# Attention on one Trainium2 core: GpSimd's two divisions of a pair of tiles as one two-array step

## The chip, the core and the metric

One core of one Trainium2 chip runs the whole program in one launch. The metric is the device time in microseconds, the median of three runs: 733.76 us before (733.6 to 734.52). An execution under the hardware profiler gives the rows that are quoted. Names in them: PE is TensorE (matmul), PEld its weight loads, DVE is VectorE, ACT is ScalarE, POOL is GpSimd, SP is SyncE; `L777` is line 777 of the kernel.

## The reference

Three blocks follow each other: windowed attention, a normalised feed-forward block with a residual, and a gated block with a short convolution. Only the first is touched by the change.

```
scores = scale * q @ k^T                     # 4 batches, 8 heads, 576 positions, 64 columns
scores = where(0 <= i - j < 128, scores - slope_h * |i - j|, -1e9)
attn   = exp(scores - max(scores))
attn   = attn / (sum(attn) + 1e-9)           # the division in question
x      = attn @ v                            # to (4, 576, 512)
x      = x + relu(layer_norm(x) * g @ w1) @ w2
h      = relu(x @ w_in);  out = (h * sigmoid(conv3(h))) @ w_out
```

## The kernel before

The 576 positions of two batches make nine tiles of 128 rows, the middle one half of each batch. With 2 pairs of batches, 4 pairs of heads and 9 tiles there are 72 tiles of two heads each; the kernel takes them in pairs (36), and two pairs, `a` and `b`, in each turn of its main loop (18 turns).

For a pair TensorE turns q and k (`turn_qk`, `L711`), and makes the scores of two tiles and two heads against 256 keys (`scores`, `L737`). Since the window is 128 wide, each row keeps just one of the two keys that lie 128 apart: VectorE joins the two halves with a mask (`join`, `L748`) and takes the minimum of the negated scores (`minima`, `L752`). ScalarE makes the exponentials, one step for each tile and head, and their sums (`exponentials`, `L762`). Then comes `shares`: VectorE adds 1e-9 (`L770`), takes the reciprocal (`L771`), and the four arrays of 128 columns are multiplied by their reciprocals, the two of the even head by VectorE (`L775`, one step of 256 columns), the two of the odd head by GpSimd (`L777`, two steps of 128 columns). The shares lie as `pp[row, tile, head, 128]`, so one head's two arrays are 256 columns apart, and its two reciprocals two columns apart.

After that TensorE turns the shares (`turn_p`, `L787`), ScalarE copies them from PSUM (`copy_p`, `L792`), GpSimd makes the two masked halves (`select_p`, two steps of 512 columns, `L799`), TensorE multiplies by v (`values`, `L815`), and ScalarE stores the result as x (`outputs`, `L828`).

Beside attention the same engines turn weights of the feed-forward block into the form that TensorE wants: GpSimd rescales (`L358`), VectorE shifts and merges bits (`L373`, `L378`, `L383`) and makes a low part (`L415`), ScalarE a high part (`L412`). Towards the end of attention the first layer norm is made too: GpSimd subtracts the mean (`L507`, 384 columns), VectorE makes low parts (`L449`).

Each engine takes its instructions in the order in which the program issues them, written out by hand in the main loop for this part of the kernel; between engines they wait on semaphores. `shares(b)` of one turn is issued in the middle of the next one, `shares(a)` at its own turn's end. A planner with costs and due times sets the order of the later blocks alone.

Of the kernel before, what the change touches and what calls it, by code (L numbers as in the profile page):

```python
# [14 lines left out]
ALU = mybir.AluOpType  # L15
PSUM = bass.MemoryType.PSUM

P = 128
# [192 lines left out]
def tile_kernel(  # L211
# [28 lines left out]
    V, S, G, T = nc.vector, nc.scalar, nc.gpsimd, nc.tensor  # L240
# [296 lines left out]
    with ExitStack() as actx:  # L537
# [110 lines left out]
        def blhs_f(kind: int, a: int = 0):  # L648
            return blhs[:, kind, a:].bitcast(F32)

        V.tensor_scalar(
            out=blhs[:, 0, :], in0=cf[:, P:W], scalar1=er[0], scalar2=er[1], op0=ALU.mult, op1=ALU.add
        )
        V.tensor_scalar(out=cb[:, 3:4], in0=er[0], scalar1=-1.0, scalar2=None, op0=ALU.mult)
        for i, r, base in ((1, 2, 3), (2, 3, 3), (0, 4, 1)):
            V.scalar_tensor_tensor(
                out=cb[:, i : i + 1], in0=er[r], scalar=BIG, in1=cb[:, base : base + 1],
                op0=ALU.mult, op1=ALU.add,
            )
        for i in range(4):  # L660
            cs = slice(i * D, (i + 1) * D)
            V.tensor_scalar(
                out=b0[:, cs], in0=cf[:, cs], scalar1=er[1], scalar2=cb[:, i : i + 1],
                op0=ALU.mult, op1=ALU.add,
            )
        for kind, r in ((1, 2), (3, 4)):
            V.tensor_scalar(
                out=blhs[:, kind, :], in0=blhs_f(0), scalar1=er[r], scalar2=None, op0=ALU.add
# [3 lines left out]
            out=blhs[:, 2, TAIL:], in0=blhs_f(0, TAIL), scalar1=er[2], scalar2=er[3],  # L672
            op0=ALU.add, op1=ALU.add,
        )
        for pr in range(NPAIR):
            V.tensor_scalar(
                out=brhs[:, pr, :], in0=b0, scalar1=sl[:, pr : pr + 1], scalar2=None, op0=ALU.mult
# [24 lines left out]
        live = {}  # L702
# [64 lines left out]
        def shares(n: int):  # L767

            sm = live["sm", n]
            V.tensor_scalar(out=sm[:, 1], in0=sm[:, 0], scalar1=1e-9, scalar2=None, op0=ALU.add)  # L770
            V.reciprocal(out=sm[:, 1], in_=sm[:, 1])  # L771
            pp = live["pp", n].rearrange("p u h j -> p (u h) j")
            even = live["pp", n][:, :, 0, :]
            r = sm[:, 1].rearrange("p (u h) -> p u h", h=2)[:, :, 0:1].broadcast_to([P, 2, P])
            V.tensor_tensor(out=even, in0=even, in1=r, op=ALU.mult)  # L775
            for i in (1, 3):
                G.tensor_scalar(  # L777
                    out=pp[:, i, :], in0=pp[:, i, :], scalar1=sm[:, 1, i : i + 1], scalar2=1.0,
                    op0=ALU.mult, op1=ALU.mult,
                )  # L780

        def turn_p(n: int, pool=ps_t, tag="pt"):
            pp = live.pop(("pp", n))
# [78 lines left out]
        for n in range(0, NS, 4):  # L862
# [21 lines left out]
            if n > 4:  # L884
                shares(b - 4)
# [4 lines left out]
            exponentials(a)  # L890
            exponentials(b, range(2 if 0 < n and not last else 4))
            shares(a)
            if not before:
                shares(b)
# [716 lines left out]
    for s in (1, 2):  # L1611
# [6 lines left out]
        for p in range(NF1 // 2):  # L1618
            extra = []
            if s == 1:  # L1620
                g, j = 4 + p // 4, p % 4
# [297 lines left out]
```

## Time and profile before

| | before |
|---|---|
| median of three runs | 733.76 us |
| the profiled execution | 733.1 us |
| its span | 731.4 us |
| TensorE busy | 711.1 us (97%) |
| VectorE busy | 518.9 us (71%) |
| ScalarE busy | 403.1 us (55%) |
| GpSimd busy | 242.7 us (33%) |
| granted TensorE clock, mean | 0.998 |

The span is what the profile covers; the time of the execution lies 1.7 us above it. Busy times are means over very different stretches: attention fills the first 147 us, and all of GpSimd's divisions and selects lie there. A busy TensorE is not one at its peak, and the duration of a GpSimd or VectorE step holds whatever the step waited for after it had started.

### The profile page before, as it was taken

How to read it: one execution, taken by the hardware profiler on the slowest of the kernel's cores; microseconds unless marked ns; L12 is line 12 of the kernel's file. 1: busy time of each engine (PE TensorE's matmuls, PEld its weight loads, DVE VectorE, ACT ScalarE, POOL GpSimd, SP SyncE). 2: the span in 40 equal slices, each digit the busy share in tenths (PEclk: the TensorE clock that was granted, in tenths of full speed). 3: DMA queues.
4: the chain of work that ended last, by engine and by line, in shares of the span. 5: the costliest groups of instructions: out<-in, count | busy, mean ns of one | idle time of the engine just before them, and what ended most of it. 6: DMA issues, size and time to landing. Idle time of an engine off the chain costs nothing.

```text
span 731.4 us, 13425 instructions
## 1 busy us (share of the span) xinstructions
PE 711.1 (97%) x4704; PEld 663.3 (91%) x4704; DVE 518.9 (71%) x1017; ACT 403.1 (55%) x1050; POOL 242.7 (33%) x408
## 2 busy tenths in 40 slices
PE   7999988899999999999999999999999999999998
PEld 6777866799999999999999999999999899998887
DVE  6799899577888636566778655468469998786731
ACT  4888877654534323344346334344477787776741
POOL 1788889868822102221310223343421000000000
PEclk9999999999999999999999999999999999999999
DMA  6777766258539827977860689997932000000011
GB/s 152 174 184 178 193 161 188 70 159 239 172 112 293 266 70 205 304 220 246 249 190 11 190 273 290 295 276 208 261 93 81 16 30 16 30 21 23 30 49 53
DMA packets 122303, 114.63 MB, mean 157 GB/s; under 512 B 63552, under 2 KB 87292, under 8 KB 122236
## 3 DMA queue, kind: packets, MB, share of 16 engines
q1 hardware_dynamic: 101020, 76.81, 35.1%
q0 software_dynamic: 20160, 36.71, 18.2%
q8 instruction: 37, 0.61, 0.3%
q10 hardware_dynamic: 1056, 0.26, 0.2%
q14 instruction: 30, 0.25, 0.1%
HBM read 80.70 MB, written 33.05 MB: 156 GB/s over the span
## 4 chain that ended last, share of the span: by engine, by line
PE 83%; POOL 6%; DVE 5%; ACT 3%; DMA 2%; issue 1%; POOLq 0%; ACTq 0%; DVEq 0%
PE bank L1038 73%; PE ps L737 3%; POOL pt L799 2%; DMA wind<-r 2%; PE po L815 2%; POOL pp L777 2%; PE ptp L787 2%; PE ptr L711 1%; DVE ps L748 1%; DVE mn L752 1%; PE bank L1094 1%; ACT fa L999 1%; POOL xm L507 1%; ACT pp L762 1%; PE busy L611 1%
## 5 line engine op out<-in xcount | busy, mean ns | idle before, releaser
L1038 PE MATMUL bank<-hhr,r 128*128 128x384 f32 x1152 | 213.8, 337 | 0.5 <-DVE fa L1006 0.5
L1038 PE MATMUL bank<-r,r 128*128 128x288 f32 (+1 forms) x1248 | 204.0, 314 | 1.2 <-ACT fa L999 1.2
L1038 PEld LDWEIGHTS bank<-hhr,r 128*128 128x128 f32 x1152 | 199.1, 188 | 2.6 <-DVE fa L1006 1.5
L1038 PEld LDWEIGHTS bank<-r,r 128*128 128x128 f32 x1248 | 193.9, 188 | 4.4 <-ACT fa L999 2.3
L1332 POOL DMA_DIRECT2D r<-w1d x96 | 51.8, 540 | 174.3 <-PE bank L1038 161.9
L999 ACT ACTIVATE fa<-bank 128x288 f32<-128x288 f32 (+1 forms) x112 | 49.8, 444 | 72.5 <-PE bank L1038 71.2
L1038 PE MATMUL bank<-r 128*128 128x512 f32 (+2 forms) x360 | 81.8, 372 | 0.2 <-ACT r L1782 0.2
L1038 PEld LDWEIGHTS bank<-r 128*128 128x128 f32 x360 | 63.6, 188 | 9.9 <-ACT r L1782 0.7
L999 ACT ACTIVATE r<-fa 128x256 fp32r<-128x256 f32 (+2 forms) x94 | 47.9, 521 | 39.0 <-DMA wind<-r 14.4
L1006 DVE TENSOR_TENSOR fa<-bank,fa 128x288 f32<-128x288 f32 (+1 forms) x88 | 43.5, 501 | 25.1 <-ACT fa L999 13.5
L999 ACT ACTIVATE hhr<-bank 128x384 fp32r<-128x384 f32 x46 | 22.5, 490 | 69.4 <-PE bank L1038 69.3
L777 POOL TENSOR_SCALAR pp<-pp,sm 128x128 f32<-128x128 f32 x72 | 48.7, 686 | 27.9 <-DVE sm L771 26.4
L762 ACT ACTIVATE pp<-ps,mn 128x128 f32<-128x128 f32 x144 | 51.4, 383 | 11.1 <-DVE mn L752 8.8
L1014 DVE SCALAR_TENSOR_TENSOR fa<-fa,cw 128x576 f32<-128x576 f32 x64 | 51.3, 814 | 1.5 <-ACT fa L999 0.7
L1006 DVE TENSOR_TENSOR r<-fa,r 128x256 fp32r<-128x256 f32 (+1 forms) x74 | 37.7, 521 | 20.1 <-ACT r L999 14.2
L1014 DVE SCALAR_TENSOR_TENSOR hhr<-bank,hhr 128x384 fp32r<-128x384 f32 x46 | 25.5, 554 | 33.9 <-ACT hhr L999 33.7
L737 PE MATMUL ps<-kt,qt 64*128 64x256 f32 x288 | 44.9, 406 | 2.6 <-ACT pp L762 1.7
L815 PE MATMUL po<-pt,rawv 128*64 128x128 f32 x544 | 38.2, 280 | 8.0 <-POOL pt L799 5.1
L1038 PE MATMUL bank<-r,hhr 128*128 128x512 f32 (+1 forms) x192 | 44.5, 381 | 0.0
L799 POOL TENSOR_SCALAR_AFFINE_SELECT pt<-pc 128x512 f32<-128x512 f32 x72 | 43.8, 639 | 1.5 <-ACT pc L792 1.0
L815 PEld LDWEIGHTS po<-pt,rawv 128*64 128x64 f32 x544 | 28.9, 136 | 17.0 <-POOL pt L799 14.3
L999 ACT ACTIVATE fa<-fa 128x576 f32<-128x576 f32 (+1 forms) x64 | 39.0, 620 | 2.5 <-DVE fa L1006 1.4
(146 smaller groups left out, 1129.7 us busy)
## 6 DMA issues: line engine op xcount, KB each, us to landing
r<-w1d POOLq DMA_DIRECT2D x96, 256.0 KB, 4.9
fa<-in_moe_w_ch SPq DMA_DIRECT2D x24, 512.0 KB, 5.3
w1d<-r SPq DMA_DIRECT2D x40, 256.0 KB, 3.7
wind<-r SPq DMA_DIRECT2D x28, 256.0 KB, 5.8
r<-wind POOLq DMA_DIRECT2D x28, 256.0 KB, 5.1
out<-h SPq DMA_DIRECT2D x17, 256.0 KB, 2.0
rawq<-in_q SPq DMA_DIRECT2D x32, 128.0 KB, 3.5
rawv<-in_v SPq DMA_DIRECT2D x32, 128.0 KB, 2.9
```

The costliest lines, as they stand in the source:

```text
L507: G.tensor_tensor(out=y, in0=xt(g * GT, (g + 1) * GT, j), in1=bcs[g, 0], op=ALU.subtract)
L737: T.matmul(ps[:, h, u, :].rearrange("p (o j) -> p o j", o=2), lhs, rhs, start=i == 0, stop=i == 1,)
L762: S.activation(pp[:, u, h, :], sc[:, h, u], AF.Exp, bias=mn[:, h, u : u + 1], scale=-1.0, accum_out=sm[:, 0, i : i + 1],)
L777: G.tensor_scalar(out=pp[:, i, :], in0=pp[:, i, :], scalar1=sm[:, 1, i : i + 1], scalar2=1.0, op0=ALU.mult, op1=ALU.mult,)
L787: T.transpose(ptp[:, 2 * u + h, :], pp[:, u, h, :], ident)
L799: G.affine_select(out=parts[:, i], in_=pc, compare_op=ALU.is_ge, fill=0.0, base=base, pattern=[[0, 4], [sign, P]], channel_multiplier=-sign,)
L815: T.matmul(po[h * D : (h + 1) * D, u, :], rvs[bl, pr][:, t - 1 + i, h, :], pt[:, i, 2 * u + h, :], start=i == i0, stop=i == 1,)
L999: lambda: S.activation(now(out), now(src), func, **kw),
L1006: "V", tt_ns(cols(out)), lambda: V.tensor_tensor(out=out, in0=a, in1=b, op=op),
L1014: lambda: V.scalar_tensor_tensor(out=now(out), in0=now(a), scalar=sc, in1=now(b), op0=op0, op1=op1),
L1038: T.matmul(out, lhs, now(rhs), start=start and n == 0, stop=stop and n == len(items) - 1, skip_group_check=True,)
L1332: plan.add("G", 560, lambda: nc.gpsimd.dma_start(dst, src), [src], [dst], nbytes=262144)
```

## The change

In `shares` GpSimd's two steps of 128 columns with a scalar for each row become one step of 256 columns with two arrays: the odd head's shares of both tiles, and their reciprocals, each repeated over 128 columns. It is the form that VectorE has for the even head already; a loop over the two engines now writes both. The arithmetic is the same.

```diff
-            pp = live["pp", n].rearrange("p u h j -> p (u h) j")
-            even = live["pp", n][:, :, 0, :]
-            r = sm[:, 1].rearrange("p (u h) -> p u h", h=2)[:, :, 0:1].broadcast_to([P, 2, P])
-            V.tensor_tensor(out=even, in0=even, in1=r, op=ALU.mult)
-            for i in (1, 3):
-                G.tensor_scalar(
-                    out=pp[:, i, :], in0=pp[:, i, :], scalar1=sm[:, 1, i : i + 1], scalar2=1.0,
-                    op0=ALU.mult, op1=ALU.mult,
-                )
+            for h, eng in enumerate((V, G)):
+                part = live["pp", n][:, :, h, :]
+                r = sm[:, 1].rearrange("p (u h) -> p u h", h=2)[:, :, h : h + 1].broadcast_to([P, 2, P])
+                eng.tensor_tensor(out=part, in0=part, in1=r, op=ALU.mult)
```

GpSimd's queue at the two turns that the prediction works through (from 102.4 us on), before; `pp` are the shares, `sm` the sums and reciprocals, `fa` a weight, `xm` the layer norm's differences, `pt` the masked halves, and the numbers are those of the buffers:

```order
L777 TENSOR_SCALAR pp_1618<-pp_1618,sm_1619 128x128 x2
L358 TENSOR_SCALAR fa<-fa 128x512
L777 TENSOR_SCALAR pp_1730<-pp_1730,sm_1731 128x128 x2
L799 AFFINE_SELECT pt_1752<-pc_1750 128x512 x2
L799 AFFINE_SELECT pt_1818<-pc_1816 128x512 x2
L777 TENSOR_SCALAR pp_1736<-pp_1736,sm_1737 128x128 x2
L358 TENSOR_SCALAR fa<-fa 128x512
L507 TENSOR_TENSOR xm_0_1837<-x,fa 128x384
L777 TENSOR_SCALAR pp_1856<-pp_1856,sm_1857 128x128 x2
```

The same place of GpSimd's queue in the changed kernel, whose lines behind the edit are numbered five lower:

```order
L775 TENSOR_TENSOR pp_1594<-pp_1594,sm_1595 128x2x128
L358 TENSOR_SCALAR fa<-fa 128x512
L775 TENSOR_TENSOR pp_1704<-pp_1704,sm_1705 128x2x128
L794 AFFINE_SELECT pt_1725<-pc_1723 128x512 x2
L794 AFFINE_SELECT pt_1791<-pc_1789 128x512 x2
L775 TENSOR_TENSOR pp_1710<-pp_1710,sm_1711 128x2x128
L358 TENSOR_SCALAR fa<-fa 128x512
L507 TENSOR_TENSOR xm_0_1809<-x,fa 128x384
L775 TENSOR_TENSOR pp_1828<-pp_1828,sm_1829 128x2x128
```

Each two steps became one in the same place, and nothing else of this queue moved; VectorE's, ScalarE's, TensorE's and SyncE's queues hold the same instructions in the same order as before. In the changed kernel `L775` is the line of VectorE's and of GpSimd's division alike.

## Rows read from the trace of the kernel before

**Rows 1.** The page: the span, and the chain that ended last by engine.

```profile
span 731.4 us, 13425 instructions
...
PE 83%; POOL 6%; DVE 5%; ACT 3%; DMA 2%; issue 1%; POOLq 0%; ACTq 0%; DVEq 0%
```

**Rows 2.** Busy us and instructions by engine in two stretches; clock, DMA, GB/s.

```profile
20.00:147.00 127.00, 117.06 (x1226) 94.11 (x1224) 107.74 (x226) 101.08 (x401) 108.25 (x165) 1.00 0.66 163
147.00:731.40 584.40, 579.05 (x3380) 556.63 (x3377) 399.41 (x754) 292.48 (x610) 129.75 (x218) 1.00 0.51 155
```

**Rows 3.** The chain of waits, 100 to 127 us: start, us, engine, line.

```profile
106.62 0.61 DVE ps L748
...
113.43 1.39 POOL pp L777 x2
```

**Rows 4.** The chain of waits over the whole span: by line, three pieces.

```profile
by line: PE bank L1038 73.2%; PE ps L737 2.8%; POOL pt L799 2.4%; DMA wind<-r 2.4%; PE po L815 2.0%; POOL pp L777 1.8%; PE ptp L787 1.6%; PE ptr L711 1.2%; DVE ps L748 1.1%; issue 1.0%; DVE mn L752 0.9%; PE bank L1094 0.9%; ACT fa L999 0.8%
...
41.54 0.71 DVE ps L748
...
46.66 1.72 POOL pp L777 x2
...
134.10 1.37 DVE xna L449 x2
```

**Rows 5.** GpSimd's division by source line: shortest/middle/longest in ns.

```profile
L777 POOL TENSOR_SCALAR pp<-pp,sm x72: 364/535/1387, 13.0 to 139.1; 128x128 f32<-128x128 f32 x72
```

**Rows 6.** GpSimd's two-array steps by source line, the same columns.

```profile
L507 POOL TENSOR_TENSOR xm<-x,fa x4: 1002/1223/1460, 112.0 to 124.2; 128x384 f32<-128x384 f32 x4
L1236 POOL TENSOR_TENSOR r<-fa,r x20: 1299/1316/1762, 151.0 to 205.0; 128x512 fp32r<-128x512 f32 x20
```

**Rows 7.** Timeline of GpSimd, 102.4 to 115.2 us: start, us, instruction.

```profile
102.70 1.47 POOL L777 TENSOR_SCALAR pp<-pp,sm 128x128 f32<-128x128 f32 x2 [1.53 <-DVE sm L771]
104.14 0.90 POOL L358 TENSOR_SCALAR fa<-fa 128x512 f32<-128x512 f32 x1
105.02 1.83 POOL L777 TENSOR_SCALAR pp<-pp,sm 128x128 f32<-128x128 f32 x2
...
111.97 1.46 POOL L507 TENSOR_TENSOR xm<-x,fa 128x384 f32<-128x384 f32 x1
113.41 1.41 POOL L777 TENSOR_SCALAR pp<-pp,sm 128x128 f32<-128x128 f32 x2
```

**Rows 8.** Timeline of GpSimd, 102.4 to 103.75 us: a pair's first step alone.

```profile
102.70 1.12 POOL L777 TENSOR_SCALAR pp<-pp,sm 128x128 f32<-128x128 f32 x1 [1.53 <-DVE sm L771]
```

**Rows 9.** Timeline of VectorE, 102.4 to 115.2 us.

```profile
102.98 0.68 DVE L378 SCALAR_TENSOR_TENSOR fa<-fa 128x512 int32<-128x512 int32 x1
103.58 0.27 DVE L770 TENSOR_SCALAR sm<-sm 128x4 f32<-128x4 f32 x1
...
104.09 0.43 DVE L775 TENSOR_TENSOR pp<-pp,sm 128x256 f32<-128x256 f32 x1
104.44 1.14 DVE L415 TENSOR_TENSOR r<-fa,r 128x512 fp32r<-128x512 f32 x1
105.50 0.68 DVE L383 SCALAR_TENSOR_TENSOR fa<-fa 128x512 int32<-128x512 int32 x1
...
111.39 1.17 DVE L415 TENSOR_TENSOR r<-fa,r 128x512 fp32r<-128x512 f32 x1
112.48 1.49 DVE L383 SCALAR_TENSOR_TENSOR fa<-fa 128x512 int32<-128x512 int32 x1
113.90 0.41 DVE L373 TENSOR_SCALAR fa<-fa 128x512 int32<-128x512 int32 x1
```

**Rows 10.** Timelines of GpSimd and VectorE around 80.9 us.

```profile
80.88 0.67 POOL L358 TENSOR_SCALAR fa<-fa 128x512 f32<-128x512 f32 x1 [0.47 <-DMA fa<-in_moe_w_ch]
80.96 0.86 DVE L775 TENSOR_TENSOR pp<-pp,sm 128x256 f32<-128x256 f32 x1
```

**Rows 11.** Timeline of VectorE, 97 to 99.5 us: a join behind TensorE.

```profile
99.18 0.70 DVE L748 COPY_PREDICATED ps<-own,ps 128x512 f32<-128x512 int32 x1 [0.60 <-PE ps L737]
```

## The prediction

> **What bounds the kernel now.** I read the page's head first: TensorE is on 83% of the chain that ended last, GpSimd on 6%, VectorE on 5%, of 731.4 us [rows 1]. The change touches only attention, so next come the stretches. From 147 us to the end TensorE is busy 579.05 of 584.40 us; nothing of the change lies there, and it only starts earlier or later. From 20 to 147 us VectorE is busy 107.74 of 127 us and GpSimd 108.25 [rows 2]: two engines at 85%, neither with much slack, beside a TensorE that waits now and then. Whatever moves the end of this stretch moves the end of the kernel one for one, because no gap behind it is large enough to swallow it.
>
> The chain inside the stretch changes hands about every 7 us, once for each step of four tiles. In some steps it runs through VectorE up to the join (`L748`), in some through GpSimd's divisions (`L777`) and selects, in some it waits for TensorE's scores [rows 3, 4, 11]. `L777` is 1.8% of the whole chain, 13.2 us [rows 4]: of 36 pairs of divisions some nine are on it. So two questions count: how long GpSimd needs for a pair, and how long it keeps VectorE waiting meanwhile.
>
> **What a division waits for now.** `L777` takes 364 ns at best, 535 in the middle, 1387 at worst [rows 5]. The spread is waiting for VectorE, and the two timelines show it as an exclusive turn. The first division of the pair at 102.70 lasts 1.12 us, to 103.82 [rows 8]. It starts while VectorE's own division runs, and VectorE's next step `L378` also goes ahead of it, to 102.98 + 0.68 = 103.66 [rows 9]; the GpSimd step ends 0.16 us later. The second then ends at 102.70 + 1.47 = 104.17 [rows 7], so after its turn comes, the pair needs 0.51 us. The block works the other way too: `L770`, which handles four columns, starts at 103.58 and ends at 103.85, 0.03 us after the first division lets go [rows 9].
>
> **The change, part by part.** 72 one-array steps of 128 columns go; 36 two-array steps of 256 columns come, at the same places in GpSimd's queue. No DMA, queue, buffer or other engine's instruction moves.
>
> 1. The new step alone. The trace has GpSimd multiplying or subtracting two arrays at 384 and 512 columns: at best 1.002 and 1.299 us [rows 6]. That is (1.299 - 1.002) / 128 = 2.3 ns a column, so 256 columns take 1.002 - 128 x 0.0023 = 0.71 us. Two old steps at their best take 2 x 0.364 = 0.73 us [rows 5]. Alone, nothing is gained; the saved start is paid back by the second array.
>
> 2. The new step after a wait. The subtraction `L507` at 111.97 (384 columns) ends at 113.43, and VectorE's `L415` ahead of it ended at 111.39 + 1.17 = 112.56 [rows 7, 9]: 0.87 us of holding. For 256 columns I scale to 0.87 x 256 / 384 = 0.58 us. The bounds: if the repeated divisor costs nothing and the step goes at the rate of a one-array step, `L358` gives 0.52 us for 512 columns (it ends at 104.14 + 0.90 = 105.04, and VectorE's division ahead of it at 104.09 + 0.43 = 104.52) [rows 7, 9], so 0.26 us; if the repeated operand is dear, the 0.87 us of the 384 columns. No row shows a repeated operand on GpSimd. I take 0.58, the nearest two-array row. Against 0.51 for the old pair that is +0.07 us for GpSimd; in pairs whose second division had to wait as well (at 105.02, 1.83 us [rows 7]) it is a gain.
>
> [...]
>
> 3. What VectorE loses. Before, it was let in between the two divisions after 0.16 us; now it waits 0.58. `L770` ends 0.42 us later, and with it the next reciprocal and VectorE's next division.
>
> Worked through the step from 102.4 us. GpSimd's new step ends at 103.66 + 0.58 = 104.24 (before 104.17). VectorE's second division starts at 104.51 instead of 104.09, and now `L358`, started at about 104.21, is in front of it; alone `L358` takes 0.67, so until 104.88, and the division ends 0.27 us after it (as at 80.96 + 0.86 = 81.82 behind 80.88 + 0.67 = 81.55 [rows 10]), at 105.15 instead of 104.52. `L415` goes next, 0.60 us (as `L383` took: 105.50 + 0.68 = 106.18 behind 104.44 + 1.14 = 105.58 [rows 9]), to 105.75. Then GpSimd's second new step, to 106.33: before it was 105.02 + 1.83 = 106.85, so GpSimd is 0.52 us ahead. `L383` waits for that and ends 0.54 later (as behind `L507`: 112.48 + 1.49 = 113.97 against 113.43), at 106.87 instead of 106.18, and `L373` ends at 107.21 instead of 106.62: +0.59 us. The chain runs through VectorE here, straight into the join [rows 3]. So the step loses 0.59 us although GpSimd wins.
>
> The next step is GpSimd's: the first new step ends 0.07 late, `L358` wins back 0.24 because VectorE is now behind it, but `L507` lets VectorE's `L415` pass and ends 0.15 late, and the second new step, after `L373` as today (113.90 + 0.41 [rows 9]), ends at 0.15 + 0.07 = 0.22 us after 113.41 + 1.41 = 114.82 [rows 7].
>
> 4. The sum over the stretch, by who holds the chain. VectorE straight into the join, like 41.54 and 106.62 [rows 3, 4]: four steps, counting two where TensorE's scores come at about the same moment, so 0.5 each: +2.0. GpSimd with a weight step or `L507` between the pairs: three steps at 0.22: +0.66. GpSimd with a second division that waited, at 46.66: its two new steps come out about 0.25 ahead: -0.25. The step after 134.10, where VectorE's `L449` leads into the divisions and would be blocked [rows 4]: +0.4. TensorE's steps, where VectorE has been idle for it before the join, 0.60 us at 99.18 [rows 11]: VectorE has the room, 0. Together +2.8 us.
>
> The profiled execution took 733.1 us around its span of 731.4; the sum makes it 735.9. The median of the three runs is 733.76, so I predict 736.6.
>
> **Rivals.**
> - Faster: the new step runs near 0.26 us, since its divisor is two values repeated. For it: nothing in the trace has such an operand. Against: both two-array rows agree on 2.3 ns a column. Each of the nine pairs on the chain then gains 0.51 - 0.26 = 0.25 us, -2.25, and the four VectorE steps lose 0.10: 733.76 - 2.25 + 0.4 = 731.9. It decides below about 0.45 us.
> - No difference: the chain has another engine at hand within a few tenths, so that VectorE's loss counts only where it holds the chain on both sides of the join (two steps, +1.0), and GpSimd's terms stay (+0.66 - 0.25): 735.2 or less, down to the old time. For it: TensorE and VectorE alternate. Against: both engines at 85%.
> - Much slower: `L770` stands right behind the first pair in most steps, and VectorE never recovers the 0.42 us; 16 steps give +6.7: 740.5. Against: in TensorE's steps VectorE has 0.60 us to give [rows 11].
> - Turns by order of start: GpSimd's step begins when VectorE's division ends and does not let `L378` pass. GpSimd's first new step would end 0.5 us earlier and VectorE lose 0.6 in place of 0.42; four of GpSimd's pairs on the chain give -2.0, VectorE's four steps +2.4, so about 734. The trace speaks against it, since `L378` did pass [rows 8, 9]. [...]
>
> **How the numbers follow.** Forecast 0.47, much slower 0.11, no difference 0.14 and turns by order of start 0.04, faster 0.24. This kernel's measurement tells about 0.2%, 1.5 us, from nothing. So slower 0.58, within 0.2% 0.18, faster 0.24. The range reaches to just above the faster rival's time, which leaves about half of it out, and to just below the much slower one's, of which half is left out too, 0.18 in all: 732.0 to 740.0. The forecast alone would span 735.2 to 738.5.
>
> **What would show it.** In the profile after: the new GpSimd step at 0.71 us at best, and at about 1.54 us where the old pair took 1.47 (0.96 of waiting and 0.58); it ends 0.58 us after the VectorE step that it waited for. `L770` behind a pair grows from 0.27 to about 0.7 us. VectorE's busy time in attention rises, GpSimd's falls. The rest of the kernel keeps its length from attention's end to the last instruction. The forecast is wrong if the new step's best is under 0.55 us, or if `L770` keeps its 0.27.

## The result and the profile after

The changed kernel takes 745.47 us (median of 4 runs, 742.43 to 748.31), the kernel before, run beside it, 734.14 (4 runs, 733.6 to 735.25): ratio 1.0147, 95% interval 1.0124 to 1.017. It is slower, as forecast, but by 11.3 us where 2.8 were worked out, and far above the range. The profiled execution took 744.1 us around a span of 742.4.

The page of the changed kernel, span and chain by engine, as [rows 1]:

```profile
span 742.4 us, 13390 instructions
...
PE 77%; DVE 13%; ACT 4%; DMA 3%; POOL 2%; issue 2%; SPq 0%; ACTq 0%; POOLq 0%; DVEq 0%
```

VectorE's share of the chain went from 5% to 13%, GpSimd's from 6% to 2%, TensorE's from 83% to 77%. The two stretches of the changed kernel, as [rows 2], cut where attention ends (the first matmul of the next block: 147.04 us before, 156.89 now):

```profile
20.00:156.90 136.90, 119.53 (x1223) 94.85 (x1223) 123.58 (x226) 100.76 (x400) 100.65 (x131) 0.99 0.62 152
156.90:742.40 585.50, 579.27 (x3379) 556.56 (x3377) 400.36 (x754) 291.92 (x610) 130.23 (x218) 1.00 0.51 155
```

Attention is 9.85 us longer, the rest 1.1 us. From 20 us to attention's end VectorE is busy 123.58 us for 107.74 with the same 226 instructions, GpSimd 100.65 for 108.25. GpSimd did get lighter; VectorE waits inside its own steps. Which ones, the groups by line show: busy us and mean ns, VectorE, up to attention's end. Before:

```profile
L383 DVE SCALAR_TENSOR_TENSOR fa<-fa 128x512 int32<-128x512 int32 x12 | 11.4, 951 | 0.0
L415 DVE TENSOR_TENSOR r<-fa,r 128x512 fp32r<-128x512 f32 x12 | 10.7, 895 | 0.0
L378 DVE SCALAR_TENSOR_TENSOR fa<-fa 128x512 int32<-128x512 int32 x12 | 8.6, 719 | 0.0
L770 DVE TENSOR_SCALAR sm<-sm 128x4 f32<-128x4 f32 x36 | 8.0, 222 | 1.6 <-ACT pp L762 1.6
L373 DVE TENSOR_SCALAR fa<-fa 128x512 int32<-128x512 int32 x12 | 5.4, 450 | 1.1 <-POOL fa L358 1.1
```

The same groups after:

```profile
L415 DVE TENSOR_TENSOR r<-fa,r 128x512 fp32r<-128x512 f32 x12 | 13.2, 1102 | 0.0
L378 DVE SCALAR_TENSOR_TENSOR fa<-fa 128x512 int32<-128x512 int32 x12 | 13.2, 1101 | 0.0
L383 DVE SCALAR_TENSOR_TENSOR fa<-fa 128x512 int32<-128x512 int32 x12 | 12.9, 1076 | 0.0
L770 DVE TENSOR_SCALAR sm<-sm 128x4 f32<-128x4 f32 x36 | 11.1, 307 | 1.9 <-ACT pp L762 1.9
L373 DVE TENSOR_SCALAR fa<-fa 128x512 int32<-128x512 int32 x12 | 9.8, 814 | 0.0
```

`L378` +4.6, `L373` +4.4, `L770` +3.1, `L415` +2.5, `L383` +1.5: together 16.1 us, as much as VectorE's busy time grew from the start to attention's end (119.54 to 135.60 us). Its join and minimum, which read PSUM, stayed as they were (690 and 692 ns before, 685 and 692 after). The chain of the changed kernel, 109 to 115 us, runs through just these:

```profile
109.24 1.02 DVE fa L378
110.26 0.56 DVE sm L770
...
111.48 1.02 DVE r L415
112.50 1.04 DVE fa L383
113.54 0.77 DVE fa L373
114.31 0.61 DVE ps L748
```

The same turn on GpSimd, as [rows 7], and on VectorE, as [rows 9] (start, us, instruction; steps of one engine overlap in these rows: `L378` starts at 109.16, 0.08 us before the division ahead of it ends at 109.24):

```profile
108.87 0.85 POOL L775 TENSOR_TENSOR pp<-pp,sm 128x256 f32<-128x256 f32 x1 [1.96 <-DVE sm L771]
109.69 1.10 POOL L358 TENSOR_SCALAR fa<-fa 128x512 f32<-128x512 f32 x1
111.20 0.76 POOL L775 TENSOR_TENSOR pp<-pp,sm 128x256 f32<-128x256 f32 x1 [0.41 <-ACT pp L762]
111.91 3.48 POOL L794 TENSOR_SCALAR_AFFINE_SELECT pt<-pc 128x512 f32<-128x512 f32 x4
```

```profile
108.82 0.42 DVE L775 TENSOR_TENSOR pp<-pp,sm 128x256 f32<-128x256 f32 x1
109.16 1.10 DVE L378 SCALAR_TENSOR_TENSOR fa<-fa 128x512 int32<-128x512 int32 x1
110.19 0.63 DVE L770 TENSOR_SCALAR sm<-sm 128x4 f32<-128x4 f32 x1
...
111.06 0.42 DVE L775 TENSOR_TENSOR pp<-pp,sm 128x256 f32<-128x256 f32 x1
111.40 1.10 DVE L415 TENSOR_TENSOR r<-fa,r 128x512 fp32r<-128x512 f32 x1
112.42 1.11 DVE L383 SCALAR_TENSOR_TENSOR fa<-fa 128x512 int32<-128x512 int32 x1
113.46 0.85 DVE L373 TENSOR_SCALAR fa<-fa 128x512 int32<-128x512 int32 x1
```

Read the ends. VectorE's division ends at 109.24, GpSimd's new step at 109.72, 0.48 later; it did not let `L378` pass, as the old step had [rows 8, 9]. `L378` ends at 110.26, 0.54 after it; GpSimd's `L358` at 110.79, 0.53 after that; `L770` at 110.82. Here the engines take turns, one step each, and VectorE pays 0.42 us at `L378` (1.10 for 0.68) and 0.47 at `L770` (0.63 for 0.16). At the end of the turn it is the same with `L415` beside the division (1.10 for 0.68) and `L383` and `L373` beside the selects (1.11 for 0.68, 0.85 for 0.41): four selects take 3.48 us here, 2.40 in the same turn before, where they began only at 106.81, when these steps were over. From the reciprocal of pair `b` to the end of `L373` it was 4.20 us before (102.42 to 106.62) and is 5.70 now (108.61 to 114.31).

### The profile page after: what moved, and what is told of

Read it like the earlier page. It is cut to its first block, busy times and chain, and to the rows that moved or that the text cites. A ratio compares the mean times of both kernels' runs of the same rounds, so it can differ in the third digit from the quotient of the medians.

```text
span 742.4 us, 13390 instructions
## 1 busy us (share of the span) xinstructions
PE 713.2 (96%) x4704; PEld 663.7 (89%) x4704; DVE 536.0 (72%) x1017; ACT 402.6 (54%) x1050; POOL 235.7 (32%) x372
## 4 chain that ended last, share of the span: by engine, by line
PE 77%; DVE 13%; ACT 4%; DMA 3%; POOL 2%; issue 2%; SPq 0%; ACTq 0%; POOLq 0%; DVEq 0%
PE bank L1033 72%; DVE ps L748 2%; DVE fa L378 2%; POOL pt L794 1%; DVE pp L775 1%; DVE fa L383 1%; DVE mn L752 1%; ACT pp L762 1%; DVE r L415 1%; PE ps L737 1%; DMA wind<-r 1%; DMA fa<-in_moe_w_in 1%; PE bank L1089 1%; PE po L810 1%; DVE fa L373 1%
## 5 line engine op out<-in xcount | busy, mean ns | idle before, releaser
L794 POOL TENSOR_SCALAR_AFFINE_SELECT pt<-pc 128x512 f32<-128x512 f32 x72 | 55.3, 798 | 1.6 <-ACT pc L787 1.0
L810 PE MATMUL po<-pt,rawv 128*64 128x128 f32 x544 | 39.8, 284 | 9.8 <-POOL pt L794 7.4
L775 POOL TENSOR_TENSOR pp<-pp,sm 128x256 f32<-128x256 f32 x36 | 28.7, 799 | 46.7 <-DVE sm L771 41.6
```

What stands on the lines that cost most here:

```text
L775: eng.tensor_tensor(out=part, in0=part, in1=r, op=ALU.mult)
L794: G.affine_select(out=parts[:, i], in_=pc, compare_op=ALU.is_ge, fill=0.0, base=base, pattern=[[0, 4], [sign, P]], channel_multiplier=-sign,)
L810: T.matmul(po[h * D : (h + 1) * D, u, :], rvs[bl, pr][:, t - 1 + i, h, :], pt[:, i, 2 * u + h, :], start=i == i0, stop=i == 1,)
```

## The experiments

Theory 1, in several forms, is that VectorE's waits make the loss: the old step lets a second VectorE step by, the new one takes the very next turn. The rivals: the length of the new step (theory 2); its two-array form; GpSimd's finishing too early, so that its selects meet VectorE's weight steps (theory 3); VectorE's load as such. A hold is the time from the end of VectorE's step to the end of the GpSimd step that waited for it; SBUF is the memory in which this kernel keeps its shares, PSUM the one in which it keeps its scores. All edits are in `shares` unless said otherwise.

The table that the readings rest on: mean ns of VectorE's four weight steps (12 each up to attention's end) and of `L770`; `sum` is the four together, one turn's weight work; `idle` is VectorE's wait for TensorE's scores ahead of the join; `selects` are the four selects in the turn near 107 us (two and two in `e7_odd_undivided`). Times that are not in the table stand in the text.

| kernel | median us (before beside it) | L378 | L415 | L383 | L373 | sum | L770 | selects us | idle us | attention's end |
|---|---|---|---|---|---|---|---|---|---|---|
| before | 734.14 | 719 | 895 | 951 | 450 | 3015 | 222 | 2.40 | 10.3 | 147.04 |
| after | 745.47 (734.14) | 1101 | 1102 | 1076 | 814 | 4093 | 307 | 3.48 | 6.4 | 156.89 |
| e1_mid | 735.59 (733.84) | 1100 | 721 | 744 | 457 | 3022 | 285 | 2.39 | 10.0 | 148.65 |
| e2_end | 740.16 (733.84) | 684 | 1342 | 1105 | 806 | 3937 | 233 | 3.03 | 7.2 | 152.15 |
| e3_two_tt | 735.36 (733.84) | 887 | 988 | 865 | 679 | 3419 | 251 | 3.03 | 8.1 | 149.96 |
| e4_const | 731.73 (733.84) | 777 | 904 | 799 | 563 | 3043 | 202 | 3.02 | 8.1 | 144.31 |
| e5_const_wide | 737.39 (734.07) | 892 | 890 | 1041 | 796 | 3619 | 264 | 3.47 | 6.9 | 150.02 |
| e8_half | 737.45 (734.07) | 888 | 888 | 1040 | 795 | 3611 | 291 | 3.48 | 8.4 | 151.75 |
| e7_odd_undivided | 736.51 (733.78) | 722 | 1080 | 1001 | 598 | 3401 | 238 | 1.41 + 1.53 | 9.1 | 150.81 |
| e11_spacer | 737.21 (733.78) | 1100 | 1170 | 818 | 484 | 3572 | 191 | 2.58 | 6.9 | 149.65 |
| e12_one_old | 731.33 (733.78) | 684 | 817 | 728 | 588 | 2817 | 196 | 3.02 | 10.6 | 145.52 |
| e14_spacer_end | 736.78 (734.54) | 1100 | 1104 | 784 | 449 | 3437 | 268 | 2.58 | 6.8 | 149.43 |

**One position at a time.** The new step for the pair in the middle of the turn alone (`e1_mid`), and for the pair at its end alone (`e2_end`):

```diff
+            if n % 4 == 2:            # e2_end: n % 4 == 0
+                G.tensor_tensor(out=odd, in0=odd, in1=rep(1), op=ALU.mult)
+            else:
...                                    # the two old steps
```

> Only the divisions of pair b, which are issued in the middle of the next turn just ahead of VectorE's L378, take the two-array step; those of pair a keep the two old steps. Theory 1 (order of turns: the two-array step takes its turn right after VectorE's own division and before VectorE's next step, which the old step let pass; from there both engines alternate) expects L378 near 1.1 us and L770 behind it longer than 0.27, but the weight steps behind pair a nearly as before, so a third to a half of the change's loss: +3 to +6 us, 737 to 740. Theory 2 (length of the hold: 0.56 us instead of 0.16 costs, whoever goes first) expects half: +5.5, about 739.5. Theory 3 (the selects, which come earlier behind pair a, collide with VectorE's weight steps, and that is the loss) expects nearly nothing here: +0 to +2, 734 to 736.

> Only the divisions of pair a, behind which GpSimd's selects come, take the two-array step; those of pair b keep the two old steps. Theory 1 expects half or more of the loss: +5 to +8, 739 to 742. Theory 2 expects half: +5.5, about 739.5. Theory 3 expects nearly all of it: +8 to +11, 742 to 745, with select steps of 1.08 us as in the changed kernel.

Middle: ratio 1.0017 (1.0001 to 1.0033), +1.7 us; end: 1.008 (1.0051 to 1.0109), +6.3. The end position is the dear one. In the middle `L378` pays 0.38 us, but the old steps at the end then meet less: the sum stays 3022. The two together are 8.0 us, not 11.3: the positions feed each other. No theory has both times: 735.59 lies where theory 3 put it (theory 1 had 737 to 740, though `L378` is at the 1.1 us that it names), 740.16 where theory 1 put it (theory 3 had 742 to 745).

**Two short two-array steps** in place of one:

```diff
+            for u in range(2):
+                G.tensor_tensor(out=odd[:, u], in0=odd[:, u], in1=rep(1)[:, u], op=ALU.mult)
```

> The form alone: GpSimd's division as two two-array steps of 128 columns. Theory 1 expects the first of them to end about 0.2 us after VectorE's division, with L378 waiting 0.2 us (0.85 to 0.9 us long), and no first step of 1.12 us any more; time well above before, 738 to 745. Theory 2 expects the holds of 0.28 us to cost about a third of the change's loss: 736 to 738, with L378 still passing the first step.

1.0023 (1.0005 to 1.0041). Both ranges missed, 738 to 745 and 736 to 738. `L378` is at 887, so the first step does go ahead of it, and costs it 0.20 us over the 684 where it goes first, about half of the 0.42 after; with the second short step ahead of them the four selects take 3.03 us, for 3.48 after.

**What lets VectorE by: the scalar read through a pointer, or the number of arrays?** One-array steps with a constant, two of 129 columns (`e4_const`) or one of 258 (`e5_const_wide`); the reciprocals go to a column of their own in the shares' tile so that all waits stay. Against the kernel before, other lines left out:

```diff
-                    out=pp[:, i, :], in0=pp[:, i, :], scalar1=sm[:, 1, i : i + 1], scalar2=1.0,
+                    out=pp[:, u, 1], in0=pp[:, u, 1], scalar1=0.25, scalar2=1.0,
# e5_const_wide, in place of the new step:
+                out=pp[:, :, 1], in0=pp[:, :, 1], scalar1=0.25, scalar2=1.0,
```

> The odd head is multiplied by a constant, not by its reciprocal: two steps of 129 columns with one array and no scalar read through a pointer; the reciprocal stands in column 129, so that the steps wait for the same instruction as before. Theory 1, in the form that the old step asks late because it reads its scalar through a pointer first, expects the first step to take its turn ahead of L378 and to last 0.5 to 0.6 us where it lasted 1.12; GpSimd's selects then come earlier, and the time lies above before, 735 to 740. If the old step is late only because it is short or has one array, it still lets L378 pass and the time is that of before, 734 +- 1.5. Theory 2 expects the time of before as well, since the hold is as short.

> The odd head is multiplied by a constant in one one-array step of 2 x 129 columns: one step, asking at once for its turn as in e4_const, holding about 0.27 us where the changed kernel's holds 0.48 to 0.56. Theory now (length in one piece: a long GpSimd step that goes ahead of VectorE's makes every VectorE step with two arrays in SBUF wait that long, and the two engines then go step by step) expects a time between e4_const and the two steps of e3_two_tt, 730 to 736, with L378 at about 0.85 to 0.9 us. Rival (it is the one-piece form as such, one step instead of two, that brings the selects forward into VectorE's weight steps) expects 739 or more.

`e4_const`: 0.9973 (0.9954 to 0.9992); `e5_const_wide`: 1.0042 (1.0023 to 1.0061), between the two ranges. VectorE's `L378` in a turn of `e4_const`, and its GpSimd division by line:

```profile
108.88 0.78 DVE L378 SCALAR_TENSOR_TENSOR fa<-fa 128x512 int32<-128x512 int32 x1
```

```profile
L777 POOL TENSOR_SCALAR pp<-pp x72: 290/531/749, 13.5 to 136.4; 128x129 f32<-128x129 f32 x72
```

`L378` waits here, 777 in the mean against 684 where it goes first (`e2_end`, `e12_one_old`), and no step takes over 749 ns, where the old one, with its pointer, took 1.12 us [rows 8]. One array and a constant go ahead too: in these runs it is the pointer that lets a VectorE step by, not the single array. That part of the theory held; its time did not (735 to 740 expected): as a short step goes first, VectorE pays little (0.09 us at `L378`), and GpSimd's step takes 550 ns in the mean for the old one's 686, 0.27 us less a pair.

**The length.** The new step over half its columns, 2 x 64:

```diff
+                c = P if eng is V else P // 2
+                eng.tensor_tensor(out=part[:, :, :c], in0=part[:, :, :c], in1=r[:, :, :c], op=ALU.mult)
```

> GpSimd's two-array step takes just 2 x 64 of the 2 x 128 columns; the other half of the odd head stays undivided. The form is that of the change, the hold half as long, about 0.25 to 0.28 us. Theory (length in one piece) expects 730 to 736, about that of e5_const_wide, with L378 at 0.85 to 0.9 us. Rival (two arrays read at once are the trouble, whatever the length) expects 739 or more, with L378 still near 1.1 us.

1.0045 (1.0032 to 1.0059), above the 730 to 736 expected, with `L378` where it was expected. VectorE's division and GpSimd in a turn of `e8_half`:

```profile
108.07 0.42 DVE L776 TENSOR_TENSOR pp<-pp,sm 128x256 f32<-128x256 f32 x1
108.21 0.54 POOL L776 TENSOR_TENSOR pp<-pp,sm 128x128 f32<-128x128 f32 x1 [0.41 <-DVE sm L771]
108.71 3.48 POOL L795 TENSOR_SCALAR_AFFINE_SELECT pt<-pc 128x512 f32<-128x512 f32 x4
```

The same in a turn of `e5_const_wide`:

```profile
106.25 0.43 DVE L775 TENSOR_TENSOR pp<-pp 128x256 f32<-128x256 f32 x1
106.40 0.55 POOL L776 TENSOR_SCALAR pp<-pp 128x258 f32<-128x258 f32 x1 [0.42 <-DVE pp L772]
106.90 3.47 POOL L797 TENSOR_SCALAR_AFFINE_SELECT pt<-pc 128x512 f32<-128x512 f32 x4
```

`L378` and `L415` pay 0.21 us less each than after, 12 times: 5.1 us, and attention ends 5.14 earlier. Yet this kernel, with half the division left out, is still 3.4 us slower than before: `L383` and `L373` still meet the selects (3.48). So length alone does not explain it. `e5_const_wide`, one array of as many columns as the new step, holds 0.27 us (106.68 to 106.95) where `e8_half` holds 0.26 (108.49 to 108.75), half of the new step's 0.48, and comes out at the same time. So the two-array form is not the trouble: at the same hold one array costs as much as two.

**GpSimd with nothing to divide** (`e7_odd_undivided`: the odd head's steps are taken out), and **VectorE with all of it** (`e6_vector_all`: one step of 512 columns):

```diff
-                G.tensor_scalar(... for i in (1, 3))           # e7: both gone (shortened)
+            V.tensor_tensor(out=pp, in0=pp, in1=r, op=ALU.mult)   # e6: r repeated to 4 x 128
```

> GpSimd makes no division at all; the odd head stays undivided. Theory of turns: GpSimd's rescale and selects come earlier still and meet VectorE's weight steps, which takes back part of the work saved: 730 to 738, with VectorE's weight steps still at 1.1 us behind them. Rival (GpSimd's divisions themselves are what costs): 1.352 us a pair gone from a GpSimd that is busy 85% of attention, 722 to 729.

> VectorE divides all four arrays of a pair in one step of 512 columns (0.69 us instead of 0.43), GpSimd none; the arithmetic is complete. Theory of turns: VectorE gets 36 x 0.26 = 9.4 us more work, and GpSimd's selects come earlier as in e7_odd_undivided; slower than before, 737 to 747. Rival (fewer steps that fight for the turn make up for it): 728 to 734, faster than both kernels.

`e7`: 1.0031 (1.0016 to 1.0046). Without any division GpSimd's work is less by 1.35 us a pair, and the kernel is 2.7 us slower than before: `L415` is at 1080 beside the selects, which come earlier; `L383` is at 1001, but `L378` and `L373` are not near the 1.1 us expected. `e6`: 746.96 us, 1.0182 (1.0158 to 1.0207); VectorE's division takes 781 ns for 456 there, 11.7 us in all. Both times lie where the theory of turns put them: taking GpSimd's divisions away altogether gains nothing here.

**The weight steps out of the way.** The weight steps of the turn's end (`L415`, `L383`, `L373`) are issued in the next turn behind the minima instead, in the changed kernel (`e9_moved_tt`) and in the one before (`e10_moved_old`); edit in the main loop:

```diff
             minima(b)
+            if before:
+                extras(n - 4, 1)
...
-            extras(n, 1)
```

> The changed kernel with the weight and layer-norm steps that stood at the end of each turn (VectorE's L415, L383, L373 behind pair a's division) issued in the next turn instead, behind both joins and minima. Behind pair a's division VectorE then has its join and minimum, which read PSUM. Theory (GpSimd's step makes VectorE's steps with two arrays in SBUF wait) expects most of the loss to go: 734 to 740, and no L415 or L383 of 1.1 us behind a division. Rival (the changed kernel is late because of its own chain through GpSimd, not because of VectorE's waits) expects 743 or more.

> The same move in the kernel before, with the two old steps. Its own effect: the theory expects within 1% of before, 728 to 739, and the distance between e9_moved_tt and this one at most 4 us where it is 11 us between the changed kernel and before. The rival expects the distance to stay at about 11 us.

767.06 and 771.11 us: both absolute times missed, since the move itself costs 21.6 us in the changed kernel and 37 in the one before. What it tells is the distance: with these steps away from the end-of-turn division the new step is 4 us faster than the old ones in the median (766.83 to 771.74 against 769.17 to 772.23, which overlap), not 11 slower. That fits theory 1, but it is weak support: VectorE waits 41.0 and 49.0 us for TensorE's scores in these two, so a wait of its own costs little in either, and TensorE, busy 102 and 103 of the 127 us from 20 to 147 us, got a granted clock of 0.91 in the mean there (117 us and 1.00 before).

**Work added to GpSimd.** A step of four columns with a pointer scalar, into a tile `sp` that nobody reads, behind each new step (`e11_spacer`), or behind the one at the turn's end alone (`e14_spacer_end`):

```diff
                 eng.tensor_tensor(out=part, in0=part, in1=r, op=ALU.mult)
+            if n % 4 == 0:                                  # e14_spacer_end only
+                G.tensor_scalar(out=sp, in0=sm[:, 0], scalar1=sm[:, 1, 1:2], scalar2=1.0,
+                                op0=ALU.mult, op1=ALU.mult)
```

> The changed kernel with a short extra step behind each two-array step on GpSimd: four columns times a scalar read through a pointer, into a tile that nobody reads. Work is added. Theory (step-for-step turns: with one division step GpSimd's long rescale and selects of 512 columns stand right behind it and take every second turn from VectorE's weight steps; the second old step used to take one such turn for 0.1 to 0.16 us and so held the long ones back) expects it faster than the changed kernel's 745.5 in spite of the added work: 737 to 743, with L770 at 0.2 to 0.3 us and fewer selects of 1.08 us. Rival (the length of the two-array step's own hold, 0.48 us, is all of the loss) expects 745 or more.

> The changed kernel with the short extra step only behind pair a's division at the end of a turn, in front of the selects. If the harm is done where the selects stand right behind the division, most of the 8 us comes back: 737 to 740. If it is the rescale behind the middle division, or both alike, half or less: 741 to 744.

1.0053 (1.003 to 1.0076) and 1.0037 (1.002 to 1.0055): of 11.3 us, 7.9 and 9.1 come back by adding work, the first as expected, the second a little more than the 737 to 740 allowed. GpSimd and VectorE in a turn of `e14_spacer_end`:

```profile
106.31 0.75 POOL L775 TENSOR_TENSOR pp<-pp,sm 128x256 f32<-128x256 f32 x1 [0.42 <-ACT pp L762]
107.06 1.21 POOL L778 TENSOR_SCALAR sp<-sm 128x4 f32<-128x4 f32 x1
108.22 2.58 POOL L799 TENSOR_SCALAR_AFFINE_SELECT pt<-pc 128x512 f32<-128x512 f32 x4
```

```profile
106.52 1.10 DVE L415 TENSOR_TENSOR r<-fa,r 128x512 fp32r<-128x512 f32 x1
107.54 0.68 DVE L383 SCALAR_TENSOR_TENSOR fa<-fa 128x512 int32<-128x512 int32 x1
108.14 0.41 DVE L373 TENSOR_SCALAR fa<-fa 128x512 int32<-128x512 int32 x1
```

Four columns take 1.21 us: the step ends at 108.27, 0.05 after `L383` (108.22), having let `L415`'s rest and all of `L383` by. The selects start behind it and meet little. `L415` is as slow as after (1104); only `L383` (1076 to 784) and `L373` (814 to 449) are faster, 12 x 0.657 = 7.9 us, and attention ends 7.46 earlier. This is the cleanest of the experiments: of the four weight steps it moves these two alone (`L770` falls too, from 307 to 268).

**One old step less** (`e12_one_old`, tile 1's odd head undivided), and **that head divided by ScalarE** in the kernel before (`e13_scalar`):

```diff
-            for i in (1, 3):
+            for i in (1,):
...
+            S.activation(pp[:, 3, :], pp[:, 3, :], AF.Copy, scale=sm[:, 1, 3:4])   # e13 only
```

> The kernel before with its second old step on GpSimd left out (the odd head of the pair's second tile stays undivided). Work is taken away, and no step is longer than before. The theory of turns expects it slower than before all the same, since the rescale and the selects now stand right behind one short step: 735 to 740, with selects of 1.08 us. The rival (length of the hold alone) expects it not slower: 730 to 734.

> The kernel before, with the second tile's odd head divided by ScalarE (128 columns, its scale read from the reciprocals) and the first tile's by GpSimd's old step; the arithmetic is complete. If the gain of one step less on GpSimd survives, 730 to 733, better than both kernels. If ScalarE, whose queue then waits for VectorE's reciprocals, comes onto the chain, 735 to 745.

`e12`: 0.9959 (0.994 to 0.9977): the theory of turns had 735 to 740 and missed, 731.33 lies where the rival put it. GpSimd and VectorE in a turn of `e12_one_old`:

```profile
102.22 1.11 POOL L777 TENSOR_SCALAR pp<-pp,sm 128x128 f32<-128x128 f32 x1 [1.58 <-DVE sm L771]
103.94 1.06 POOL L777 TENSOR_SCALAR pp<-pp,sm 128x128 f32<-128x128 f32 x1
104.97 3.02 POOL L799 TENSOR_SCALAR_AFFINE_SELECT pt<-pc 128x512 f32<-128x512 f32 x4
```

```profile
102.49 0.69 DVE L378 SCALAR_TENSOR_TENSOR fa<-fa 128x512 int32<-128x512 int32 x1
104.17 0.68 DVE L415 TENSOR_TENSOR r<-fa,r 128x512 fp32r<-128x512 f32 x1
104.77 0.77 DVE L383 SCALAR_TENSOR_TENSOR fa<-fa 128x512 int32<-128x512 int32 x1
105.47 0.85 DVE L373 TENSOR_SCALAR fa<-fa 128x512 int32<-128x512 int32 x1
```

Each pair's remaining step still lets a VectorE step by: the first ends 0.15 us after `L378`, the second 0.15 after `L415`. The selects come even earlier than in the changed kernel (3.03 us behind the reciprocal of pair `b`, 3.30 there, 4.39 before), yet the sum is the lowest of the table, and the time too. So GpSimd's being early does no harm by itself. `e13`: 778.82 us, 1.0609 (1.0553 to 1.0665), outside both ranges. The gain does not survive: ScalarE now waits in its queue for VectorE's reciprocals. Its waits, us in total, times, longest:

```profile
ACT pp L781 <- DVE sm L771: 52.3, 17, 4.9
```

No kernel that computes everything beat the one before; `e4_const` and `e12_one_old` are faster with arithmetic left out.

## Why the prediction was wrong in size

**The failed step** stands in the step worked through under point 3, and in the 0.96 us of waiting under "What would show it": "GpSimd's new step ends at 103.66 + 0.58", that is, behind `L378`. The trace had shown `L378` passing [rows 8, 9], but for a step with a pointer scalar; the changed one has none. It goes first, VectorE pays at `L378`, and GpSimd's contended step takes 0.85 and 0.76 us where 1.54 was expected. `e4_const` shows that the pointer makes the difference (no step over 749 ns, `L378` at 777), `e14_spacer_end` that a pointer step of four columns yields (1.21 us) as the one of 128 did (1.12). The kernel got slower, as forecast, and VectorE's wait is the reason, as in point 3; but the wait was put in another place and in too few turns.

**What follows from it was priced with the wrong sign.** The rival "turns by order of start" (0.04) had the mechanism, and booked GpSimd's lead as -2.0 us, for 734; the sum of point 4 has no term for the selects. In the changed kernel they come earlier and meet `L383` and `L373`, with no step ahead of them that lets VectorE by. `e14_spacer_end` puts such a step back and recovers 7.46 us of attention's 9.85; `e7_odd_undivided` has the lead without any division and loses 2.7 us. The lead alone is not the cause: `e12_one_old` and `e4_const` have it too and are 2.4 and 2.1 us faster than before, the one with steps that still yield, the other with short holds. What a kernel loses goes roughly by what its weight steps lose, the sum column. Order of start does not settle who goes first: the new step, started at 108.87 ahead of `L378` at 109.16, does (0.48 us, and `L378` 1.10); the old pointer step, started at 102.70 ahead of `L378` at 102.98, does not (1.12 us, `L378` passed).

**The count of turns.** I put +0.5 us on four VectorE turns and nothing on TensorE's, where VectorE had 0.60 us to spare [rows 11]. The loss falls on all 12 turns with weight steps, 1.08 us each in the sum column. With `L770` that makes the 16.1 us. VectorE's idle time up to attention's end went from 27.50 to 21.29 us, 3.9 of it at the scores (10.3 to 6.4): that cover of 6.2 us was used up, and the rest, 9.85, came out. The rival "much slower" had such a count (16 steps), at 0.42 us each.

**Right**: the new step alone, 673 ns at best (0.71 worked out), so nothing is gained there; `L770` behind a pair, 0.27 to 0.63 us (0.7); VectorE's busy time up, GpSimd's down; the rest of the kernel nearly the same length (+1.1 us). Neither of the two signs of being wrong appeared (673 ns, 0.63 us), because neither asks who goes first; the 1.54 us of the contended step did, and did not come.

```profile
L775 POOL TENSOR_TENSOR pp<-pp,sm x36: 673/788/847, 13.4 to 148.3; 128x256 f32<-128x256 f32 x36
```

This line answers [rows 5]. The 364 to 1387 ns spread of the old step has become 673 to 847: what looked like GpSimd's loss was VectorE's right of way.

**Open.** Why a pointer step yields is not shown, only that it does, at 4 and at 128 columns. The 2.2 to 3.4 us that remain in `e11_spacer`, `e14_spacer_end` fit `L378` and `L415`, which still pay, but were not taken away one by one. `e4_const` is faster than its sum lets expect; that GpSimd's 0.27 us a pair count there, where the chain runs through GpSimd (`L777` 9.8% of it from 95 to 150 us), is likely, not tested. `e4_const`, `e5_const_wide`, `e7_odd_undivided`, `e8_half` and `e12_one_old` leave arithmetic out, so they tell of causes, not of usable kernels.

## What to carry to other kernels

Where two engines take turns, the time that a step waits can be what lets the other engine work, as here the old step's 1.12 us, in which `L378` went by: before shortening it, ask which of them the end of the stretch depends on, and what the freed engine starts next. Read a contended step's order from its own form of instruction; a row of another form, here that of the pointer step [rows 8], did not tell who goes first. Test a gain in such a place by an idle step put back, and by taking the work out in part and altogether, and read the other engine's steps each time. Taking all of it out is no bound: here it lost 2.7 us, while taking half of it out gained 2.4.

## What the runs showed of the hardware

- A GpSimd step whose scalar is read through a pointer let a further VectorE step by: the old division took 1.12 us [rows 8] where it needs 0.364 at best [rows 5], the four-column step 1.21 (`e14_spacer_end`). Steps without one took the next turn, and ended this long after the VectorE step ahead of them: two arrays at 256 columns 0.48 us, at 128 columns 0.26 (`e8_half`), a constant at 258 columns 0.27 (`e5_const_wide`), the rescaling 0.53, a select 0.49 (111.91 + 1.08 = 112.99 behind `L415`, which ended at 112.50).
- Under such turns VectorE's step of four columns took 0.63 us for 0.16, and steps of 512 columns 1.10 for 0.68; steps with one array waited as those with two did (`L770` 0.47 us, `L373` 0.44, `L378` 0.42). The join and the minimum, which read PSUM, kept their 0.69 us (690 and 692 ns before, 685 and 692 after).
- A repeated second operand cost GpSimd nothing visible: 256 columns took 0.673 us at best, where the rows with two full arrays (1.002 us for 384 columns, 1.299 for 512 [rows 6]) make it 0.71 by a straight line, an estimate.
